# Gates in two passes, the slope by ScalarE's derivative, phases as 16-bit halves, and two sets of PSUM evictions on VectorE

## Chip, core and metric

The kernel runs on one core of a Trainium2 chip. TensorE multiplies matrices, VectorE and ScalarE work element by element, GpSimd does a little of that and issues DMAs, and SyncE issues most DMAs. The metric is device time in microseconds (us) of one execution; lower is better.

## What is computed

A forward and a backward pass over x of shape 2048 x 512 (bf16):

```python
xn = _layernorm(x)
s = _A_ref(xn, ...)            # a long convolution, kernel K from a diagonal state-space model
g = _silu(_B_ref(xn, w1, w2))  # o = silu(xn @ w1) @ w2 ; g = silu(o)
return x + s * g
```

`_A_ref` forms K[d, l] = Re sum_n C dt B exp(dt A l) for 512 channels and 2048 places, and convolves it with xn by Fourier transforms. The outputs are the result and the gradients of x, of the eight state-space parameters and of the two weights, for a given `grad_out`. For the gates the backward pass needs two things: ds = grad_out * silu(o), the gradient of the convolution's output, and do = grad_out * s * silu'(o), the gradient of the feed-forward output.

## The kernel before

The kernel is written with a tile framework. The code yields work in small steps, and generators are woven together by fixed weights (`interleave`, `woven`, `paced`). A planner then sets the order on each engine at build time, from an estimate of when each instruction's inputs and buffers are ready, with the order of the code as priority. On the chip each engine and each DMA queue works through its list in order.

The stages, by the profile's time:

- Up to about 44 us: loads, constants, layer norm. GpSimd builds the selection matrices `SEL`, ScalarE the magnitudes `mag`.
- 44 to 258 us, the table stage. `gen_tables` runs for four blocks b of 128 channels, each in two halves h. A half forms phases `V` (int32) on VectorE in two groups of 16 and 15 exponents: a product `tau * e`, a shift by a quarter turn for the cosine (L435), and a shift left by 32 - PB bits (L436), so that a turn wraps at 32 bits. ScalarE takes the sine (`sn`, L438), VectorE multiplies by `mag` into `E`, `Y` and `H`, and TensorE multiplies `Y` by `W` into `ps_k`. ScalarE evicts that to `Xr`. At the end of a block TensorE gathers `Xr` by selection matrices into two groups of `ps_e` (one PSUM buffer, pool `pt`), and twelve copies write them, some broadcast, into `KE` (`ev`, `evk`: ScalarE). Four DMAs on ScalarE's queue (L507) write `KE` to DRAM (`Kd`). The forward convolution of the block before (`gen_conv_fwd`: Kb, two Fourier stages, product with U, two inverse stages, `S_b`, stored to `Sd`) and the forward feed-forward (`gen_ffn_fwd`, in chunks of 256 rows, 0.58 steps for each step of the tables) are woven in. The feed-forward stores each chunk of o to DRAM (`Od`, by GpSimd's queue).
- 258 to about 312 us, the gate stage. The table buffers are freed; `ds` and the pool `gate` (Gr, g, u, S) take their place. The forward convolution of block 3, the last feed-forward chunk and the gates (`gen_gate_rows`, eight chunks c of 256 rows) are woven. `k.do` lies over the space of the table `Y` (the trace names it YD). A chunk whose o came while the tables still stood is loaded from `Od` into `k.do`; a chunk that comes after (`k.late`) is read from its buffer `ob`. For each chunk the gates take g = silu(o) (three buffers), store g to DRAM (`Gd`), take tanh(o/2), form ds, and build the slope from tanh and g by five VectorE instructions, then multiply by Gr and by S for blocks 0 to 2. Block 3's S_b follows at L1162.
- Meanwhile W1 and W2 are turned in place (`turned_in_place`: eight transposes in TensorE into a PSUM bank, one eviction, seven times for each). The evictions go by `evw`, pattern "AD": ScalarE and VectorE in turn.
- From about 299 us: `gen_conv_bwd`. `forward(0)` transforms ds (it needs all chunks); four steps of it are drawn before `gen_ffn_da`. Then its products (L347 to L354) with U and K, the backward feed-forward (ps_da, L925 and L927), the first output (`gen_out`), and after that the state-space gradients, the weight gradients and the layer norm's backward pass, up to 703.6 us.

The DMA buffers of the Fourier stages come by tags: `w8` (four buffers), and from the backward pass on also `w8b` (two), which take turns by a fixed cycle.

Of the kernel before, what the change touches and what calls it, by code (L numbers as in the profile page):

```python
# [10 lines left out]
ACT = mybir.ActivationFunctionType  # L11
ALU = mybir.AluOpType
F32 = mybir.dt.float32
BF16 = mybir.dt.bfloat16
I32 = mybir.dt.int32
DRAM = bass.MemoryType.DRAM
PSUM = bass.MemoryType.PSUM
P = 128
PI_LO = 3.1415925
PB = 18  # L20


BR, SR = 1.8, 0.5
# [392 lines left out]
def gen_tables(k, b):  # L416

    nc, tbl = k.nc, k.tbl
# [3 lines left out]
    for h in range(2):  # L422
        hs = slice(b * P + 64 * h, b * P + 64 * h + 64)
        mag = tbl.tile([P, NX, 64], BF16, name="mag", tag="mag")
        nc.sync.dma_start(mag[:].rearrange("p e d -> p (e d)"), k.Md[2 * b + h])
        E = tbl.tile([P, 2, 16, NE, 4], BF16, name="E", tag="E")
        Y = k.Y[h]
        H = tbl.tile([P, 2, 16, 3, 4], BF16, name="H", tag="H")
        qe = lambda ap: ap.rearrange("p e (q a) -> p e q a", a=4)
        eq = lambda ap: ap.rearrange("p q e a -> p e q a")  # L430
        for (x0, n) in ((0, 16), (16, 15)):
            V = tbl.tile([P, 2, 16, 64], I32, name="V", tag="tv", bufs=2)
            TT(out=V[:, 1, 0:n], in0=k.tau[:, hs].unsqueeze(1).to_broadcast([P, n, 64]),
               in1=k.ecst[:, x0:x0 + n].unsqueeze(2).to_broadcast([P, n, 64]), op=ALU.mult)
            TS(out=V[:, 0, 0:n], in_=V[:, 1, 0:n], scalar=-float(1 << (PB - 2)), op=ALU.add)  # L435
            TS(out=V[:, :, 0:n], in_=V[:, :, 0:n], scalar=32 - PB, op=ALU.logical_shift_left)  # L436
            sn = tbl.tile([P, 2, 16, 64], BF16, name="sn", tag="ts", bufs=2)
            nc.scalar.activation(out=sn[:, :, 0:n], in_=V[:, :, 0:n], func=ACT.Sin, scale=-2 * PI_LO / 2.0 ** 32)  # L438
            yield
            for c in range(2):  # L440
                if x0 == 0:
                    parts = ((E[:, c, :, 0:16, :], 0, 16),)
                else:
                    parts = ((E[:, c, :, 16:NE, :], 0, 5), (Y[:, c, :, 1:8, :], 5, 12), (H[:, c], 12, 15))
                for o, i0, i1 in parts:
                    TT(out=eq(o), in0=qe(sn[:, c, i0:i1]), in1=qe(mag[:, x0 + i0:x0 + i1, :]), op=ALU.mult)
                yield
        nc.sync.dma_start(k.Ed[b, h], E[:].rearrange("p c q e a -> p (c q e a)"))
# [12 lines left out]
        for q0 in range(0, 16, 8):  # L461
            W = tbl.tile([P, 4, 8, NE, 4], BF16, name="W", tag="W", bufs=2)
            g = (hs.start + 4 * q0) // 32
            for m, ec in ((0, 0), (2, 1)):
                ct = k.CT[:, g, ec:ec + 2, :].rearrange("p m (q a) -> p (m q) a", a=4).unsqueeze(2).to_broadcast([P, 16, NE, 4])
                e = E[:, ec, q0:q0 + 8].rearrange("p q e a -> p (q e a)").unsqueeze(1).to_broadcast([P, 2, 8 * NE * 4])
                TT(out=W[:, m:m + 2].rearrange("p m q e a -> p (m q) e a"), in0=e, in1=ct, op=ALU.mult)  # L467
            for u in range(2):
                ps = k.pt.tile([P, 4, 84], F32, name="ps_k", tag="pt")
                for q in range(4):  # L470
                    for m in range(4):
                        nc.tensor.matmul(out=ps[:, q], lhsT=Y[:, m % 2, q0 + 4 * u + q].rearrange("p j a -> p (j a)"),  # L472
                                         rhs=W[:, m, 4 * u + q].rearrange("p e a -> p (e a)"), start=(m == 0), stop=(m == 3))
# [10 lines left out]
                i += 1  # L484
    KE = tbl.tile([P, 8, 8, 32], BF16, name="KE", tag="W", bufs=2)
    bc = lambda ap, n: ap.unsqueeze(2).to_broadcast([P, ap.shape[1], n, 32])
    ev = k.evk
    A = k.pt.tile([P, 16, 32], F32, name="ps_e", tag="pt")
    group(A[:], [(0, 0, 16)])
    ev(KE[:, 0], A[:, 8:16])  # L490
# [61 lines left out]
def gen_ffn_fwd(k):  # L552
    nc, fp = k.nc, k.fp
    D, FT, DK, T = k.D, k.FT, k.DK, k.T
    for c in range(T // 2):
# [20 lines left out]
            yield  # L576
        if c == T // 2 - 1:
            turned_in_place(k, k.W1, k.evw)
        ob = fp.tile([P, 2, D], BF16, name="ob", tag="ob", bufs=2)
        for t in range(2):  # L580
            ps = k.pf.tile([P, D], F32, name="ps_o", tag="pf")
            for ft in range(FT):
# [1 line left out]
                                 start=(ft == 0), stop=(ft == FT - 1))  # L584
            k.evf(ob[:, t], ps[:])
            yield
        k.st(k.Od[:, 2 * c:2 * c + 2, :], ob[:])
        k.rows_done = c + 1
        if k.late:
            k.ob[c] = ob  # L590

def gen_gate_rows(k, gp, lag):

    nc = k.nc
    TT = nc.vector.tensor_tensor
    last = k.T // 2
    Gr = gp.tile([P, k.T, k.D], BF16, name="Gr")
    for t in range(0, k.T, 4):  # L600
        nc.sync.dma_start(Gr[:, t:t + 4, :], k.g_v[:, t:t + 4, :])
    for c in range(last):
        while k.rows_done <= c or (c not in k.ob and k.rows_done < min(c + 1 + lag, last)):
            yield
        ts = slice(2 * c, 2 * c + 2)
        o = k.do[:, ts, :]
        src = o
        if c in k.ob:
            src = k.ob.pop(c)[:]
        else:  # L610
            nc.sync.dma_start(o, k.Od[:, ts, :])
        G = Gr[:, ts, :]
        S = gp.tile([P, 3, 2, P], BF16, name="S", tag="S", bufs=4)
        nc.sync.dma_start(S[:].rearrange("p b t d -> p b (t d)"), k.Sd[0:3, :, 256 * c:256 * c + 256].rearrange("b p n -> p b n"))
        if src is o:
            yield
        g = gp.tile([P, 2, k.D], BF16, name="g", tag="g", bufs=3)
        nc.scalar.activation(out=g[:], in_=src, func=ACT.Silu)
        nc.sync.dma_start(k.Gd[:, ts, :], g[:])
        nc.scalar.activation(out=o, in_=src, func=ACT.Tanh, scale=0.5)  # L620
        TT(out=k.ds[:, ts, :], in0=G, in1=g[:], op=ALU.mult)

        nc.vector.tensor_scalar(out=o, in0=o, scalar1=-0.5, scalar2=0.5, op0=ALU.mult, op1=ALU.add)
        u = gp.tile([P, 2, k.D], BF16, name="u", tag="u", bufs=2)
        nc.vector.tensor_scalar(out=u[:], in0=g[:], scalar1=1.0, scalar2=-1.0, op0=ALU.mult, op1=ALU.add)
        TT(out=o, in0=o, in1=u[:], op=ALU.mult)
        nc.vector.tensor_single_scalar(out=o, in_=o, scalar=1.0, op=ALU.add)
        TT(out=o, in0=o, in1=G, op=ALU.mult)
        o3 = o[:, :, 0:3 * P].rearrange("p t (b d) -> p b t d", b=3)
        TT(out=o3, in0=o3, in1=S[:], op=ALU.mult)  # L630
        yield
# [413 lines left out]
def kernel(ctx, tc, A_u, A_A_re, A_A_im, A_B_re, A_B_im, A_C_re, A_C_im, A_log_dt, A_Dskip, B_x, B_w1, B_w2, grad_out,  # L1045
           out_0, out_1, out_2, out_3, out_4, out_5, out_6, out_7, out_8, out_9, out_10, out_11):
    nc = tc.nc
# [32 lines left out]
    k.pc = ctx.enter_context(tc.tile_pool(name="pc", bufs=2, space=PSUM))  # L1080
    k.pt = ctx.enter_context(tc.tile_pool(name="pt", bufs=1, space=PSUM))
    k.evk, k.evc, k.evf, k.evb, k.evv = (Evac(nc, "A") for _ in range(5))
    k.evx, k.evw, k.evq = Evac(nc, "D"), Evac(nc, "AD"), Evac(nc, "D")

    k.st = nc.gpsimd.dma_start
    k.const = pool("const")
# [63 lines left out]
    k.rows_done, k.late, k.ob = 0, False, {}  # L1150
    ffn = gen_ffn_fwd(k)
    paced(chain(), ffn, 0.58)
    es_t.close()
    k.late = True
    k.ds = pool("ds", side="right", es=es_x).tile([P, 16, D], BF16, name="ds")
    es_g = es_x.enter_context(ExitStack())
    gates = gen_gate_rows(k, pool("gate", side="right", es=es_g), 1)

    interleave([gen_conv_fwd(k, 3), ffn, gates], [1, 3, 1])
    for t in (slice(0, 8), slice(8, 16)):  # L1160
        last = k.do[:, t, 3 * P:4 * P]
        nc.vector.tensor_tensor(out=last, in0=last, in1=k.S_b[:, t], op=ALU.mult)  # L1162
# [4 lines left out]
    k.dftb = SimpleNamespace(tile=lambda shape, dt, name, tag: base.tile(shape, dt, name=name, tag=next(turn) if tag == "w8" else tag))  # L1167
# [48 lines left out]
```

## Time and profile before

| | before |
|---|---|
| three runs | 702.93, 706.72, 713.55 us |
| median | 706.72 us |
| span of the profiled execution | 703.6 us (no other time is listed for it) |
| busy TensorE, VectorE, ScalarE, GpSimd | 597.5, 534.5, 465.3, 85.6 us |
| mean granted TensorE clock | 0.958 |
| DMA | 148.81 MB, mean 211 GB/s |

Busy time is a share of the whole span; the stages differ much, so it has to be read stage by stage. Each row of a group of instructions gives the line, engine, operation, output and input tiles with shapes and the count, then busy us, the mean of one in ns, and the idle us of the engine just before them with what ended it. Back-to-back instructions overlap a little, so that the busy time of a full queue is less than count times mean.

### The profile page before, as it was taken

The page shows a single profiled execution, that of the slowest core. Times are in us where ns is not written, and L with a number is a line of the kernel's source. Part 1 is how long each engine was busy: PE and PEld are TensorE (multiplying, and loading weights), DVE is VectorE, ACT ScalarE, POOL GpSimd, SP SyncE. Part 2 cuts the span into 40 slices and gives each one's busy share as a digit, 9 for nine tenths or more (in the row PEclk, how much of TensorE's full clock was granted, in tenths as well). Part 3 has the DMA queues.
Part 4 walks back from the last instruction along what each step waited for, and adds up shares of the span by engine and source line. Part 5 has one row for each costly group of instructions (what it writes and reads, how often), then busy time and mean ns, then how long its engine had stood idle before and what let it go on. Part 6 is the DMA issues. An engine that isn't in the chain of part 4 may idle for free.

```text
span 703.6 us, 14464 instructions
## 1 busy us (share of the span) xinstructions
PE 597.5 (85%) x5884; PEld 436.8 (62%) x5884; DVE 534.5 (76%) x952; ACT 465.3 (66%) x626; POOL 85.6 (12%) x165
## 2 busy tenths in 40 slices
PE   0675988779999997549988999988998989999988
PEld 0454656466667675337675666756777767755877
DVE  6988995979979958999685969626679774755950
ACT  6877666779878888877664765615728665645431
POOL 2355200000000000000000000000001020123220
PEclk9998998899999999779999999999999999999999
DMA  9955453825835779598857545479989999337993
GB/s 280 342 139 201 150 192 143 329 77 211 306 120 217 288 245 310 175 295 264 275 166 226 184 172 180 129 155 226 249 202 252 197 235 232 110 116 254 288 229 99
DMA packets 158771, 148.81 MB, mean 211 GB/s; under 512 B 79280, under 2 KB 136112, under 8 KB 155120
## 3 DMA queue, kind: packets, MB, share of 16 engines
q1 hardware_dynamic: 145664, 125.07, 62.3%
q0 software_dynamic: 6144, 17.83, 6.7%
q10 hardware_dynamic: 6896, 4.98, 2.2%
q8 instruction: 46, 0.75, 0.4%
q14 instruction: 21, 0.17, 0.1%
HBM read 65.14 MB, written 64.36 MB: 184 GB/s over the span
## 4 chain that ended last, share of the span: by engine, by line
issue 74%; POOL 8%; DVE 8%; PE 4%; DMA 4%; ACT 1%; SPq 0%; POOLq 0%; DVEq 0%
PE ps_w L986 2%; POOL Hd L575 1%; DMA dh_tok<-DHd 1%; DVE st L269 1%; POOL out_dram L842 1%; POOL rstd L273 1%; DVE jk L1019 1%; POOL SEL L220 1%; DVE o L1029 1%; DMA out_dram<-gout 1%; PE ps_o L583 1%; DMA out_dram<-o 1%; DVE xn L279 1%; POOL out_dram L971 1%; PE ps_h L566 1%
## 5 line engine op out<-in xcount | busy, mean ns | idle before, releaser
L44 ACT CAST dA<-ps_s 128x1024 bf16<-128x1024 f32 x96 | 93.6, 1027 | 16.2 <-PE ps_s L298 10.2
L925 PE MATMUL ps_da<-doT,W 128*128 128x256 bf16 x448 | 62.5, 280 | 5.7 <-DVE dhT L927 5.7
L44 ACT CAST dB<-ps_i 128x1024 bf16<-128x1024 f32 x48 | 47.3, 1027 | 29.2 <-PE ps_i L327 24.4
L772 DVE TENSOR_TENSOR Tp<-Vb,Eb 128x1344 bf16<-128x1344 bf16 x64 | 51.9, 853 | 18.5 <-ACT Vb L44 7.9
L927 DVE TENSOR_TENSOR dhT<-ps_da,dhT 128x512 bf16<-128x512 f32 x56 | 37.8, 686 | 34.2 <-PE ps_da L925 29.3
L566 PE MATMUL ps_h<-XT,W 128*128 128x256 bf16 x448 | 62.1, 284 | 0.6 <-DVE XT L45 0.4
L583 PE MATMUL ps_o<-W,aT 128*128 128x512 bf16 x224 | 56.9, 390 | 3.5 <-ACT aT L574 1.6
L327 PE MATMUL ps_i<-I,sp_in 128*128 128x256 bf16 x384 | 51.4, 279 | 8.0 <-DVE sp_in L350 4.9
L936 PE MATMUL ps_dx<-W,dhT 128*128 128x512 bf16 x224 | 54.1, 379 | 0.0
L925 PEld LDWEIGHTS <-W 128*128 128x128 bf16 x448 | 43.0, 100 | 16.7 <-issue 10.8
L986 PE MATMUL ps_w<-dh_tok,xn 128*128 128x256 bf16 x448 | 49.7, 272 | 3.6 <-DMA dh_tok<-DHd 3.5
L968 PE MATMUL ps_w<-YD,a_tok 128*128 128x512 bf16 x224 | 51.5, 379 | 0.0
L566 PEld LDWEIGHTS <-W 128*128 128x128 bf16 x448 | 43.2, 102 | 12.3 <-issue 5.5
L986 PEld LDWEIGHTS <-xn 128*128 128x128 bf16 x448 | 43.6, 98 | 9.8 <-issue 4.5
L327 PEld LDWEIGHTS <-sp_in 128*128 128x128 bf16 x384 | 36.7, 100 | 20.9 <-DVE sp_in L350 8.2
L44 ACT CAST Vb<-ps_v 128x672 bf16<-128x672 f32 x64 | 42.3, 725 | 10.7 <-PE ps_v L762 10.6
L44 ACT CAST o<-ps_w 128x256 bf16<-128x256 f32 (+1 forms) x42 | 17.7, 439 | 46.4 <-PE ps_w L986 16.9
L314 PE MATMUL ps_s<-dB,F 128*64 128x512 bf16 x192 | 33.6, 418 | 12.2 <-DVE dB L45 6.5
L298 PEld LDWEIGHTS <-TF 128*128 128x128 bf16 x384 | 26.7, 102 | 24.4 <-issue 18.6
L583 PEld LDWEIGHTS <-aT 128*128 128x128 bf16 x224 | 21.3, 100 | 29.4 <-issue 9.3
L45 DVE COPY dB<-pt_f 128x2048 bf16<-128x2048 bf16 x24 | 28.7, 1218 | 12.5 <-PE pt_f L304 12.4
L472 PE MATMUL ps_k<-W,YD 128*128 128x84 bf16 x512 | 29.4, 210 | 9.6 <-DVE W L467 7.7
(231 smaller groups left out, 1304.5 us busy)
## 6 DMA issues: line engine op xcount, KB each, us to landing
Yd<-YD SPq DMA_DIRECT2D x8, 1024.0 KB, 4.5
sp_in<-Ud SPq DMA_DIRECT2D x8, 1024.0 KB, 7.4
h_in<-Hd SPq DMA_DIRECT2D x14, 512.0 KB, 4.3
Ed<-E SPq DMA_DIRECT2D x8, 672.0 KB, 4.1
Eb<-Ed SPq DMA_DIRECT2D x8, 672.0 KB, 5.2
Hd<-hT POOLq DMA_DIRECT2D x8, 512.0 KB, 6.0
Ud<-dA SPq DMA_DIRECT2D x4, 1024.0 KB, 8.1
KXd<-dA SPq DMA_DIRECT2D x4, 1024.0 KB, 5.2
```

The source lines that it names most:

```text
L44: return self.nc.scalar.copy(out=out, in_=in_)
L314: nc.tensor.matmul(out=ps[64 * h:64 * h + 64, 4 * v:4 * v + 4], lhsT=k.F2[:, c, :], rhs=Bv[:, u, h, 4 * v:4 * v + 4, :], start=True, stop= ...
L327: nc.tensor.matmul(out=ps[:, g], lhsT=Y[:, c, g0 + g, :], rhs=k.I2[:, c].rearrange("p c m -> p (c m)"), start=(c == 0), stop=(c == 1))
L472: nc.tensor.matmul(out=ps[:, q], lhsT=Y[:, m % 2, q0 + 4 * u + q].rearrange("p j a -> p (j a)"), rhs=W[:, m, 4 * u + q].rearrange("p e a - ...
L566: nc.tensor.matmul(out=ps[:, j], lhsT=k.W1[:, dk, ft * P:ft * P + P], rhs=XTv[:, :, dk, :], start=(dk == 0), stop=(dk == DK - 1))
L583: nc.tensor.matmul(out=ps[:], lhsT=aT[:, ft, t * P:t * P + P], rhs=k.W2[:, ft, :], start=(ft == 0), stop=(ft == FT - 1))
L772: k.nc.vector.tensor_tensor(out=Tp[:, c, :, r ^ c].rearrange("p e (q w) a -> p q w e a", w=2), in0=Vb[:, :, c].rearrange("p q w (e a) -> p ...
L925: nc.tensor.matmul(out=ps[:, j], lhsT=k.W2[:, ft, dk * P:dk * P + P], rhs=dTv[:, :, dk, :], start=(dk == 0), stop=(dk == DK - 1))
L927: nc.vector.tensor_tensor(out=dh[:, i0:i0 + 2, :], in0=ps[:], in1=dh[:, i0:i0 + 2, :], op=ALU.mult)
L936: nc.tensor.matmul(out=ps[:], lhsT=dhs[ft // 8][:, ft % 8, t * P:t * P + P], rhs=k.W1[:, :, ft * P:ft * P + P], start=(ft == 0), stop=(ft ...
L968: nc.tensor.matmul(out=ps[:], lhsT=at[:, t, :], rhs=k.do[:, t, :], start=(t == 0), stop=(t == k.T - 1))
L986: nc.tensor.matmul(out=ps[:], lhsT=k.xn[:, t, dk * P:dk * P + P], rhs=dh[:, t].rearrange("p j n -> p (j n)"), start=(t == 0), stop=(t == k ...
```

## The change

It does these things:

- Phases keep 16 bits for a turn (PB 18 to 16). The shift left is gone; the sine reads the low 16-bit half of each 32-bit phase.
- The twelve `KE` copies of a block go by `evw`, and `evw` is VectorE alone, so the copies of turned W1 and W2 go there too.
- Late chunks of o are evicted straight into `k.do`, and are not stored to `Od`.
- The gates are split. Pass one (`gen_gate_rows`) loads o where needed, takes g, stores it and forms ds. Pass two (`gen_slope_rows`) loads S, takes silu'(o) in place by ScalarE's Derivative_silu, and multiplies by Gr and S.
- Pass two is drawn in turn with the first four steps of the backward convolution, which now come ahead of the turning of W2. The cycle of buffers is turned by two places to match.

```diff
-PB = 18
+PB = 16
...
-            TS(out=V[:, :, 0:n], in_=V[:, :, 0:n], scalar=32 - PB, op=ALU.logical_shift_left)
+            low = V[:].bitcast(I16).rearrange("p c e (d w) -> p c e d w", w=2)[:, :, 0:n, :, 0]
...
-            nc.scalar.activation(out=sn[:, :, 0:n], in_=V[:, :, 0:n], func=ACT.Sin, scale=-2 * PI_LO / 2.0 ** 32)
+            nc.scalar.activation(out=sn[:, :, 0:n], in_=low, func=ACT.Sin, scale=-2 * PI_LO / 2.0 ** PB)
...
-    ev = k.evk
+    ev = k.evw
...
-        ob = fp.tile([P, 2, D], BF16, name="ob", tag="ob", bufs=2)
+        late = k.late
+        ob = k.do[:, 2 * c:2 * c + 2, :] if late else fp.tile([P, 2, D], BF16, name="ob", tag="ob", bufs=2)
...
-        k.st(k.Od[:, 2 * c:2 * c + 2, :], ob[:])
+        if late:
+            k.ob.add(c)
+        else:
+            k.st(k.Od[:, 2 * c:2 * c + 2, :], ob[:])
         k.rows_done = c + 1
-        if k.late:
-            k.ob[c] = ob
...
         ts = slice(2 * c, 2 * c + 2)
         o = k.do[:, ts, :]
-        src = o
-        if c in k.ob:
-            src = k.ob.pop(c)[:]
-        else:
+        if c not in k.ob:
             nc.sync.dma_start(o, k.Od[:, ts, :])
-        G = Gr[:, ts, :]
+            yield
+        g = gp.tile([P, 2, k.D], BF16, name="g", tag="g", bufs=3)
+        nc.scalar.activation(out=g[:], in_=o, func=ACT.Silu)
+        nc.sync.dma_start(k.Gd[:, ts, :], g[:])
+        nc.vector.tensor_tensor(out=k.ds[:, ts, :], in0=k.Gr[:, ts, :], in1=g[:], op=ALU.mult)
+        yield
+
+
+def gen_slope_rows(k, gp):
+
+    nc = k.nc
+    TT = nc.vector.tensor_tensor
+    for c in range(k.T // 2):
+        ts = slice(2 * c, 2 * c + 2)
+        o = k.do[:, ts, :]
         S = gp.tile([P, 3, 2, P], BF16, name="S", tag="S", bufs=4)
         nc.sync.dma_start(S[:].rearrange("p b t d -> p b (t d)"), k.Sd[0:3, :, 256 * c:256 * c + 256].rearrange("b p n -> p b n"))
-        if src is o:
-            yield
-        g = gp.tile([P, 2, k.D], BF16, name="g", tag="g", bufs=3)
-        nc.scalar.activation(out=g[:], in_=src, func=ACT.Silu)
-        nc.sync.dma_start(k.Gd[:, ts, :], g[:])
-        nc.scalar.activation(out=o, in_=src, func=ACT.Tanh, scale=0.5)
-        TT(out=k.ds[:, ts, :], in0=G, in1=g[:], op=ALU.mult)
-
-        nc.vector.tensor_scalar(out=o, in0=o, scalar1=-0.5, scalar2=0.5, op0=ALU.mult, op1=ALU.add)
-        u = gp.tile([P, 2, k.D], BF16, name="u", tag="u", bufs=2)
-        nc.vector.tensor_scalar(out=u[:], in0=g[:], scalar1=1.0, scalar2=-1.0, op0=ALU.mult, op1=ALU.add)
-        TT(out=o, in0=o, in1=u[:], op=ALU.mult)
-        nc.vector.tensor_single_scalar(out=o, in_=o, scalar=1.0, op=ALU.add)
-        TT(out=o, in0=o, in1=G, op=ALU.mult)
+        nc.scalar.activation(out=o, in_=o, func=ACT.Derivative_silu)
+        TT(out=o, in0=o, in1=k.Gr[:, ts, :], op=ALU.mult)
         o3 = o[:, :, 0:3 * P].rearrange("p t (b d) -> p b t d", b=3)
         TT(out=o3, in0=o3, in1=S[:], op=ALU.mult)
         yield
...
-    k.evx, k.evw, k.evq = Evac(nc, "D"), Evac(nc, "AD"), Evac(nc, "D")
+    k.evx, k.evw, k.evq = Evac(nc, "D"), Evac(nc, "D"), Evac(nc, "D")
...
-    gates = gen_gate_rows(k, pool("gate", side="right", es=es_g), 1)
-
-    interleave([gen_conv_fwd(k, 3), ffn, gates], [1, 3, 1])
+    gp = pool("gate", side="right", es=es_g)
+    k.dftb = SimpleNamespace(tile=lambda shape, dt, name, tag: k.dft.tile(shape, dt, name=name, tag=tag))
+    bwd = gen_conv_bwd(k)
+    interleave([gen_conv_fwd(k, 3), ffn, gen_gate_rows(k, gp, 1)], [1, 3, 1])
+    interleave([itertools.islice(bwd, 4), gen_slope_rows(k, gp)], [1, 1])
...
-    turn = itertools.cycle(["w8"] * 4 + ["w8b"] * 2)
...
+    turn = itertools.cycle(["w8"] * 2 + ["w8b"] * 2 + ["w8"] * 2)
...
     turned_in_place(k, k.W2, k.evw)
-    bwd = gen_conv_bwd(k)
     out = gen_out(k, da)
-    for i in range(4):
-        next(bwd)
```

More of the change, by code (lines that the diff above doesn't have):

```diff
@@ L15 @@
 I32 = mybir.dt.int32
+I16 = mybir.dt.int16
 DRAM = bass.MemoryType.DRAM
@@ L586, in gen_ffn_fwd @@
             yield
-        k.st(k.Od[:, 2 * c:2 * c + 2, :], ob[:])
+        if late:
+            k.ob.add(c)
+        else:
+            k.st(k.Od[:, 2 * c:2 * c + 2, :], ob[:])
         k.rows_done = c + 1
-        if k.late:
-            k.ob[c] = ob
 def gen_gate_rows(k, gp, lag):
     nc = k.nc
-    TT = nc.vector.tensor_tensor
     last = k.T // 2
-    Gr = gp.tile([P, k.T, k.D], BF16, name="Gr")
+    k.Gr = gp.tile([P, k.T, k.D], BF16, name="Gr")
     for t in range(0, k.T, 4):
-        nc.sync.dma_start(Gr[:, t:t + 4, :], k.g_v[:, t:t + 4, :])
+        nc.sync.dma_start(k.Gr[:, t:t + 4, :], k.g_v[:, t:t + 4, :])
     for c in range(last):
@@ L1149, in chain @@
             yield from woven([gen_tables(k, b), gen_conv_x(k, b), gen_conv_fwd(k, b - 1)], [3, 1, 1])
-    k.rows_done, k.late, k.ob = 0, False, {}
+    k.rows_done, k.late, k.ob = 0, False, set()
     ffn = gen_ffn_fwd(k)
@@ L1165 @@
     base = dft_pool("dftb", es_x, {"cm2": 1, "xd": 1, "w8b": 2}, k.dft, side="right")
-    turn = itertools.cycle(["w8"] * 4 + ["w8b"] * 2)
-    k.dftb = SimpleNamespace(tile=lambda shape, dt, name, tag: base.tile(shape, dt, name=name, tag=next(turn) if tag == "w8" else tag))
+    turn = itertools.cycle(["w8"] * 2 + ["w8b"] * 2 + ["w8"] * 2)
+    k.dftb.tile = lambda shape, dt, name, tag: base.tile(shape, dt, name=name, tag=next(turn) if tag == "w8" else tag)
     da = pool("da", es=es_d)
     turned_in_place(k, k.W2, k.evw)
-    bwd = gen_conv_bwd(k)
     out = gen_out(k, da)
-    for i in range(4):
-        next(bwd)
     ffb = gen_ffn_da(k, da)
```

## Prediction

> **What bounds the kernel now.** I read the page first, then the waits, then a table of stretches, then the groups of VectorE and ScalarE by shape, and last the order of time from 255 to 352 us. TensorE is busy for 597.5 of 703.6 us and VectorE for 534.5, so neither is the bound everywhere; the stretches say where each is.
>
> ```profile
> DVE  6988995979979958999685969626679774755950
> PEclk9998998899999999779999999999999999999999
> ...
> 44.00:160.00 116.00, 92.39 (x933) 66.11 (x931) 96.89 (x134) 82.68 (x117) 25.73 (x29) 0.91 0.47 169
> 160.00:258.00 98.00, 94.48 (x1029) 67.17 (x1026) 88.62 (x120) 87.08 (x125) 8.60 (x11) 1.00 0.65 235
> 258.00:280.00 22.00, 17.79 (x208) 13.21 (x208) 15.53 (x26) 18.26 (x21) 0.57 (x1) 0.98 0.85 272
> 280.00:312.00 32.00, 17.02 (x143) 12.08 (x140) 31.75 (x59) 25.84 (x25) 0.00 (x0) 0.71 0.71 225
> 312.00:341.00 29.00, 25.97 (x256) 19.14 (x254) 27.41 (x39) 21.35 (x24) 2.20 (x4) 0.98 0.83 269
> 341.00:703.60 362.60, 331.97 (x3219) 247.48 (x3218) 238.38 (x471) 197.22 (x269) 35.58 (x64) 0.98 0.76 198
> ```
>
> In the stretches the columns after the length are the busy us of TensorE, its weight loads, VectorE, ScalarE and GpSimd, then the granted clock. From 280 to 312 us VectorE is busy for 31.75 of 32 us while TensorE has 17.02, at a clock of 0.71: this is the gate stage, and VectorE bounds it. From 160 to 258 us TensorE has 94.48 of 98 and bounds. After 341 us TensorE has 331.97 of 362.6, and what begins earlier there ends earlier.
>
> ```profile
> L436 DVE TENSOR_SCALAR V<-V 128x2048 int32<-128x2048 int32 x8 | 9.9, 1231 | 0.0
> L436 DVE TENSOR_SCALAR V<-V 128x1920 int32<-128x1920 int32 x8 | 9.3, 1165 | 0.0
> L626 DVE TENSOR_TENSOR YD<-YD,u 128x1024 bf16<-128x1024 bf16 x8 | 5.5, 684 | 0.0
> L630 DVE TENSOR_TENSOR YD<-YD,S 128x768 bf16<-128x768 bf16 x8 | 4.4, 551 | 1.6 <-DMA S<-Sd 1.6
> L625 DVE TENSOR_SCALAR u<-g 128x1024 bf16<-128x1024 bf16 x8 | 3.4, 420 | 0.0
> L623 DVE TENSOR_SCALAR YD<-YD 128x1024 bf16<-128x1024 bf16 x8 | 3.4, 419 | 0.0
> L627 DVE TENSOR_SCALAR YD<-YD 128x1024 bf16<-128x1024 bf16 x8 | 3.4, 419 | 0.0
> ...
> L620 ACT ACTIVATE YD<-YD 128x1024 bf16<-128x1024 bf16 x7 | 7.2, 1062 | 0.0
> L44 ACT CAST KE<-ps_e 128x128 bf16<-128x128 f32 x12 | 3.3, 342 | 0.0
> L902 ACT ACT_TABLE_LOAD x1 | 1.3, 1283 | 0.0
> ```
>
> These are the instructions that the change takes away or moves. The order of time shows how the stage ends:
>
> ```profile
> 273.38 1.08 ACT L620 ACTIVATE YD<-ob 128x1024 bf16<-128x1024 bf16 x1
> ...
> 296.78 1.07 ACT L618 ACTIVATE g<-ob 128x1024 bf16<-128x1024 bf16 x1
> ...
> 304.91 0.69 DVE L621 TENSOR_TENSOR ds<-Gr,g 128x1024 bf16<-128x1024 bf16 x1
> ...
> 318.28 0.69 DVE L347 TENSOR_TENSOR cm<-sp_in,dA 128x1024 bf16<-128x1024 bf16 x1 [1.22 <-ACT dA L44]
> ```
>
> Only one chunk is late (one `g<-ob`). Its tanh runs 23 us ahead of its silu: the planner puts whatever it holds ready first, and the silu waits for one of three g buffers. The last ds comes at 304.91, though its silu was done by 298 at the latest; ds stands in VectorE's full queue. The backward transform needs all of ds, and its first product (L347) comes at 318.28.
>
> **The change part by part.** Prices on VectorE are from start to start in a full queue: the 0.42 us form comes every 0.33 (285.38 to 285.71), the 0.68 us form every 0.60, the shift every 1.10 (a pair from 72.66, next start 74.86).
>
> *Gates.* Each of eight chunks loses L623, L625, L626 and L627: 3 x 0.33 + 0.60 = 1.6, so 12.9 us of VectorE, all in the stage that it bounds. What stays is ds, one multiply by Gr, one by S. Tanh becomes Derivative_silu: L902 takes 1913 ns for 2048 and 1492 for 1536 elements, so 1071 for 1024, against 1062: nothing. The eight loads of S (192 KB each, SP's queue) move behind all of pass one. In the old order each stood ahead of the store of its g, and the first had to wait for Sd of block 2; now Gd goes out sooner and g comes free sooner. VectorE's 1.6 us wait for S goes too: at that time it will have ds and W copies, and S loads run during the forward transform. If that cover fails, the 1.6 stays. S has four buffers, so the fifth load waits for L630 of the first chunk, and behind it on SP stand sp_in, dhT and go_g, wanted by ScalarE and VectorE only after 305; I give this nothing, with up to 3 us (half the median landing of S, 6.1) as upper end. The forward transform of block 0 now needs pass one alone, so it can overlap the tail of block 3's forward convolution.
>
> *Late o.* One chunk: two evictions go to their final place, one 256 KB store (L587, 0.57 us of GpSimd issue) is gone. GpSimd is idle in the stage (0.57 of 54 us), so nothing.
>
> *Turned weights.* Seven copies leave ScalarE (7.1 us, 1031 ns each) for VectorE at 0.60. Four are of W1, around 250 to 263 us, where VectorE waits 3.07 and 4.16 us for TensorE: no cost. Three are of W2 in the gate stage: +1.8.
>
> *Phases.* The shift goes: 16 x 1.10 = 17.6 us of VectorE. The first two are worth nothing, since VectorE then waits 1.5 us for GpSimd's SEL before YD; 14 x 1.10 = 15.4. The Sin now reads every second 16-bit word. No row shows that; ScalarE takes 1943 ns for 2048 int32 and 1923 for 2048 bf16 (L574), the nearest rows, so I take no change. Upper end: twice as long is 30 us of ScalarE, and it idles 44 us from 44 to 258; up to 10 us might show. A gain is not excluded but has no row; 0.
>
> *Selection results.* 48 copies (KE, 15.2 us) leave ScalarE for VectorE. VectorE's nearest rows that read PSUM are 686 ns for 512 and 1220 for 1024 elements: 152 ns plus 1.04 an element. For 8192 elements in 48 copies that is 15.8 us busy, about 12 start to start. Lower end, by the fp32 copy of 218 ns for 128 elements from SBUF (L818): 8 us. I take 12, since the source is PSUM. So the table stage has 3.4 us less of VectorE and 15 less of ScalarE. Here a wait is added twice: VectorE's queue stands when ps_e is not ready, and what stands behind it is the next block's V and E, for which Sin and ps_k wait; and the four Kd issues on ScalarE's queue now wait for VectorE, with Sin and hT evictions behind. As TensorE has 94.48 of 98 us in the second half, I count 2.5 us gained; ends: 7 gained, and the third rival.
>
> *Sum.* Gate stage: -12.9 - 1.6 + 1.8 = -12.7. ScalarE is next: 25.84 of 32 us busy, and it keeps its silu and slope work, about 40 us from 262 on, so it could end near 304; I give back 0.7, so -12. Table stage -2.5. Together -14.5. The span gives 703.6 - 14.5 = 689.1; the span lies near the lower of the three runs (702.93, 706.72, 713.55), and 14.5 off their median is **692.2**.
>
> **Rivals.** *Table switches eat half.* The planner holds the slope of chunk 0 ready as soon as its silu is done, while later silus wait for g buffers; the early tanh above shows that it then pulls a ready instruction ahead. Silu, Tanh and Sin alternate without a load now, and Derivative_silu needed one (L902). Each return trip costs 2 x 1283 ns of ScalarE; three trips are 7.7 us in a stage where ScalarE is next to bound: 700. Against it: g comes free sooner, and ScalarE has evictions to fill. The Trainium skill, in "ScalarE: Activation LUTs", section "Table sets: the hidden batching unit", says to do all of one set before switching, and puts a switch at some 2.7 us with its drain; the row here has 1.28 and the next start 0.23 later. By the page three trips would be 16 us and the gain gone.
>
> *The clock comes back.* At 280 to 312 us TensorE's 17.02 us of work ran at 0.71. With shorter pauses at full clock it would be 12.1, and if ScalarE then ends the stage at its floor near 304, the stage gives 5 to 6 us more: 686. For it: the clock is 1.00 wherever TensorE is kept busy. Against: ScalarE, not TensorE, comes next. The Trainium skill, "TensorE: Matmul & The Clock Gate", section "What's actually happening", ties a half clock to an idle window of about 3.4 us; the trace agrees so far that pauses of 3.7 us (288.19) and 3.1 (309.34) stand in that stretch.
>
> *VectorE stands for the selection (slower).* In block 3 the last product W ends at 246.4, the first ps_e ends at 253.6 and the last KE copy at 258.1. If the planner puts the copies right behind W, VectorE stands through 253.6 - 246.4 = 7.2 us for each of four blocks, 29 us: 692.2 + 29 = 721. It turns slower than before from 3.6 us a block. Against it: the trace has V, shifts, E and cplx products between the two, and the planner orders by readiness; for it: both ps_e groups share one PSUM buffer.
>
> **How the numbers follow.** The forecast has 0.60, with its own range 685 to 699; the clock 0.18; switches 0.10; the standing queue 0.12. A 2% step, about what a measurement of this kernel can tell from no change, is 14.1 us, so the border is 692.6. The forecast lies at it: of its 0.60 I put 0.33 beyond and 0.27 within. Faster 0.33 + 0.18 = 0.51, same 0.27 + 0.10 = 0.37, slower 0.12. The range 679 to 712 reaches below the second rival by the 7 us end of the selection, and above the first by the ends of the S loads and the Sin; most of the third stays outside.
>
> **What would show it.** Right: no L623 to L627; the last ds before 290 us instead of 304.9; the first bwd L347 near 304 to 307 instead of 318; VectorE below 90% in that stage and ScalarE above 90%; one load of Derivative_silu's table; KE copies on VectorE at about 290 ns for 128 elements; Sin at 1.9 us; 341 to the end no longer than 363 us. Wrong: more than one such load, VectorE waiting over 3 us for ps_e, Sin well over 1.94, or a tail after the gate stage that gives the gain back.

## The result and the profile after

The changed kernel takes 702.21 us (median of 20 runs) against 706.53 us for the kernel before (20 runs): a ratio of 0.9936, 95% interval 0.9907 to 0.9965, or 4.5 us (2.5 to 6.6). The forecast was 14.5 us. All ratios here compare fast runs alone, those at most 1.5% above the fastest of the same kernel, so a ratio need not be that of the two medians. The profiled execution has a span of 700.7 us against 703.6, busy TensorE 596.9 us, VectorE 519.8, ScalarE 453.9, and a mean granted clock of 0.961.

The table of stretches, with the columns of the one shown before:

```profile
44.00:160.00 116.00, 97.15 (x1038) 71.24 (x1037) 104.67 (x164) 82.87 (x100) 22.48 (x30) 0.94 0.53 190
160.00:258.00 98.00, 94.39 (x974) 65.28 (x971) 77.41 (x127) 76.81 (x96) 7.69 (x10) 1.00 0.62 221
258.00:280.00 22.00, 14.22 (x180) 10.66 (x177) 16.84 (x24) 19.21 (x22) 0.00 (x0) 0.95 0.78 264
280.00:312.00 32.00, 24.43 (x231) 18.52 (x231) 28.03 (x44) 30.58 (x31) 0.56 (x1) 0.82 0.90 294
312.00:341.00 29.00, 22.96 (x184) 15.06 (x181) 19.15 (x28) 16.53 (x18) 1.66 (x3) 0.88 0.71 218
```

Three rows carry the story. From 280 to 312 us VectorE falls from 31.75 to 28.03 us and TensorE rises from 17.02 to 24.43, but ScalarE is now at 30.58 of 32. From 312 to 341 every engine has *less* to do than before (TensorE 22.96 after 25.97, VectorE 19.15 after 27.41): something stands there. And from 44 to 160, VectorE has become fuller, 104.67 after 96.89, although the shift is gone.

The groups of the moved instructions, by shape:

```profile
L439 ACT ACTIVATE sn<-V 128x2048 bf16<-128x2048 int16 x8 | 15.4, 1930 | 2.5 <-DVE V L436 2.5
L628 ACT ACTIVATE YD<-YD 128x1024 bf16<-128x1024 bf16 x8 | 8.3, 1058 | 0.0
L628 ACT ACT_TABLE_LOAD x3 | 3.8, 1283 | 0.1
L46 DVE CAST KE<-ps_e 128x128 bf16<-128x128 f32 x12 | 3.0, 276 | 0.0
L613 ACT ACT_TABLE_LOAD x2 | 2.6, 1283 | 1.3 <-DMA Gd<-g 1.3
```

The prices of single instructions are as forecast: the sine of 16-bit halves takes 1930 ns for 2048 elements (1943 for 32-bit words before), the derivative 1058 ns, the KE copy of 128 elements 276 ns on VectorE. But the tables of ScalarE are loaded five times around silu and its derivative, not once. The order of time at the end of the gates:

```profile
286.87 1.06 ACT L613 ACTIVATE g<-YD 128x1024 bf16<-128x1024 bf16 x1
...
287.96 0.69 DVE L615 TENSOR_TENSOR ds<-Gr,g 128x1024 bf16<-128x1024 bf16 x1
...
289.76 1.28 ACT L628 ACT_TABLE_LOAD   x1
...
297.95 1.07 ACT L628 ACTIVATE YD<-YD 128x1024 bf16<-128x1024 bf16 x1
...
303.03 0.55 DVE L631 TENSOR_TENSOR YD<-YD,S 128x768 bf16<-128x768 bf16 x1
...
305.31 1.28 DVE L928 TENSOR_TENSOR dhT<-ps_da,dhT 128x512 bf16<-128x512 f32 x2
```

The lines are the last silu, the last ds, the last load, the last derivative, the last slope product with S and the first product of the backward feed-forward. The last ds comes at 287.96 (304.91 before), the last slope product at 303.03 (310.00 before), that first product, dhT, at 305.31 (318.89 before). At that point the changed kernel leads by 13.6 us. At the end of the span it leads by 2.9. Between the two lies a hole; the timeline after the gates shows it (idle time before an instruction, and what ended it, in brackets):

```profile
331.44 0.69 DVE L657 TENSOR_TENSOR go_x<-go_x,go_g 128x1024 bf16<-128x1024 bf16 x1 [4.62 <-DMA go_x<-in_A_u_dram]
...
334.53 0.40 PE L328 MATMUL ps_i<-I,sp_in 128*128 128x256 bf16 x1 [4.65 <-DVE sp_in L351]
...
337.10 1.01 ACT L45 CAST dB<-ps_i 128x1024 bf16<-128x1024 f32 x1 [7.58 <-PE ps_i L328]
...
342.34 0.69 DVE L657 TENSOR_TENSOR go_x<-go_x,go_g 128x1024 bf16<-128x1024 bf16 x1 [6.47 <-DMA go_x<-in_A_u_dram]
```

The first output is formed chunk by chunk in go_x, which has one buffer: the load of the next chunk waits until the store of the last has left. Here the store is issued at 332.43 us and takes 4.2 us in the median; the next load is issued at 336.98, and the sum that needs it starts at 342.34. VectorE stands 4.6 and 6.5 us for these loads. Behind the waiting instruction in its queue are the backward products of sp_in; TensorE waits for those, and ScalarE for TensorE. Before, VectorE also waited for this buffer (4.0 us), but TensorE had 13.84 us of work from 330 to 344; after, it has 9.47.

### The profile page after: what moved, and what is told of

Same layout as the page of the kernel before. It is cut to its first block, busy times and chain, and to the rows that moved or that the text cites. A ratio compares the mean times of both kernels' runs of the same rounds, so it can differ in the third digit from the quotient of the medians.

```text
span 700.7 us, 14417 instructions
## 1 busy us (share of the span) xinstructions
PE 596.9 (85%) x5884; PEld 437.0 (62%) x5884; DVE 519.8 (74%) x959; ACT 453.9 (65%) x575; POOL 80.9 (12%) x164
## 5 line engine op out<-in xcount | busy, mean ns | idle before, releaser
L45 ACT CAST dA<-ps_s 128x1024 bf16<-128x1024 f32 x96 | 93.4, 1034 | 14.5 <-PE ps_s L299 11.9
L926 PE MATMUL ps_da<-doT,W 128*128 128x256 bf16 x448 | 60.3, 275 | 6.0 <-DVE dhT L928 3.9
L987 PE MATMUL ps_w<-dh_tok,xn 128*128 128x256 bf16 x448 | 51.2, 278 | 5.4 <-DMA dh_tok<-DHd 5.4
L926 PEld LDWEIGHTS <-W 128*128 128x128 bf16 x448 | 42.1, 98 | 16.3 <-issue 11.5
L299 PEld LDWEIGHTS <-TF 128*128 128x128 bf16 x384 | 26.1, 101 | 20.6 <-issue 15.0
L315 PE MATMUL ps_s<-dB,F 128*64 128x512 bf16 x192 | 30.5, 388 | 6.9 <-ACT dA L45 2.6
```

Source lines behind the costliest of these rows:

```text
L45: return self.nc.scalar.copy(out=out, in_=in_)
L315: nc.tensor.matmul(out=ps[64 * h:64 * h + 64, 4 * v:4 * v + 4], lhsT=k.F2[:, c, :], rhs=Bv[:, u, h, 4 * v:4 * v + 4, :], start=True, stop= ...
L926: nc.tensor.matmul(out=ps[:, j], lhsT=k.W2[:, ft, dk * P:dk * P + P], rhs=dTv[:, :, dk, :], start=(dk == 0), stop=(dk == DK - 1))
L987: nc.tensor.matmul(out=ps[:], lhsT=k.xn[:, t, dk * P:dk * P + P], rhs=dh[:, t].rearrange("p j n -> p (j n)"), start=(t == 0), stop=(t == k ...
```

## The experiments

Each compares its kernel with the kernel before, run on the same chip in the same set of runs; the ratios are those. The median of the kernel before moved between 704.3 and 707.6 us from one set to the next, so kernels of different sets are compared by ratio.

**The two kernels again.** No edit.

> The kernel before, unchanged, once more. In the two profiles in hand the changed kernel leads by 9.5 us at the last dhT (L927, 519.1 against 509.6 us) and by 2.9 at the end, though from there on the instructions stand in the same order on every engine. Theory spread: the stretch from the last dhT to the end (184.5 us before, 191.1 after) varies by several us from execution to execution of one kernel, and the profile of before had a short one; here it is 186 to 192. Theory give-back: something in that stretch takes the lead back each time; here it is 184 to 186 again. Time 706 +- 3 by both.

Measured: 707.57 us, ratio 0.9974 (0.993 to 1.0018).

> The changed kernel, unchanged, once more. Spread: last dhT near 509.6 again, and the stretch behind it anywhere from 184 to 192 us. Give-back: the stretch is 189 to 193 again, longer than in the kernel before by 4 or more. Time 702 +- 3 by both.

Measured: 702.23 us, ratio 0.9908 (0.9864 to 0.9951); in a later set, beside three of its variants:

> The changed kernel itself, beside its three variants on one chip. It came at 702.2 in two sets, so 702 is expected here too, 0.991 to 0.994 of before. If the variants differ from it only because they ran in other sets, it comes at 695 to 697 like them; then neither the switches nor KE's move cost anything that the end sees.

Measured: 701.45 us, ratio 0.9935 (0.9898 to 0.9972). The changed kernel is 4 to 6 us faster. A quarter of a per cent, 2 us, is what the same kernel shows against itself here, and half a per cent further below, where one kernel has 0.9852 in one set and 0.9904 in another; smaller differences between sets say nothing. The stretch behind the last dhT, 191.1 us in the first trace of the changed kernel, is 184.4 in the third (184.5 before): it varies from execution to execution, as theory spread has it.

**The change cut in two.** First the new gates alone, on the changed kernel with shift, 18 bits and the evictions as before:

```diff
-PB = 16
+PB = 18
...
-    ev = k.evw
+    ev = k.evk
...
-    k.evx, k.evw, k.evq = Evac(nc, "D"), Evac(nc, "D"), Evac(nc, "D")
+    k.evx, k.evw, k.evq = Evac(nc, "D"), Evac(nc, "AD"), Evac(nc, "D")
```

> The changed kernel with the old phases (shift, PB 18), KE on ScalarE and turned weights on both engines: the gates, late o and the buffer cycle alone. If the gate stage makes the lead (theory gates), the last dhT comes 6 to 9 us before 519.1 and the time is 3 to 8 below the kernel before. If the lead is mostly the table stage's (theory tables), under 4 us at the last dhT and no time that can be told from before.

Measured: 706.88 us, ratio 1.0009 (0.9973 to 1.0044): nothing. Then the rest alone, put on the kernel before (16-bit phases, KE and turned weights on VectorE, old gates):

> The kernel before with 16-bit phases, KE and turned weights on VectorE, and the old gates. Theory gates: 1 to 4 us of lead at the start of block 3's forward convolution, and since the turned weights add to VectorE in the gate stage, 0 to 3 at the last dhT; time within 3 of before. Theory tables: 5 us or more at the last dhT, and 3 to 5 in time.

Measured: 709.18 us, ratio 1.0028 (0.9992 to 1.0065): nothing either. Neither half brings the 4 to 6 us of the whole. The timeline of the new gates alone shows why they bring nothing:

```profile
303.32 0.69 DVE L1165 TENSOR_TENSOR YD<-YD,S_b 128x1024 bf16<-128x1024 bf16 x1
304.18 1.07 ACT L628 ACTIVATE YD<-YD 128x1024 bf16<-128x1024 bf16 x1
305.13 2.84 ACT L45 COPY W<-pt_t 128x1024 bf16<-128x1024 bf16 x3
...
323.91 1.28 DVE L928 TENSOR_TENSOR dhT<-ps_da,dhT 128x512 bf16<-128x512 f32 x2
```

ScalarE takes the derivative of the last chunk at 304.18 and only then copies the turned W2 that the backward feed-forward needs: ds is 11 us earlier than before (294.3 after 304.9), yet ScalarE comes to `doT`, the transposed do that the first dhT also needs, only at 318.95. The first dhT comes at 323.9, later than the 318.9 of before.

The rest alone is ahead by 6.5 us at the last KE copy, by 7.0 at the first dhT and by 2.7 at the last one (516.4 after 519.1); what it gains in the table stage it loses behind the gates.

**Only the four VectorE instructions.** The kernel before without the lines that build the slope:

```diff
-        nc.vector.tensor_scalar(out=o, in0=o, scalar1=-0.5, scalar2=0.5, op0=ALU.mult, op1=ALU.add)
-        u = gp.tile([P, 2, k.D], BF16, name="u", tag="u", bufs=2)
-        nc.vector.tensor_scalar(out=u[:], in0=g[:], scalar1=1.0, scalar2=-1.0, op0=ALU.mult, op1=ALU.add)
-        TT(out=o, in0=o, in1=u[:], op=ALU.mult)
-        nc.vector.tensor_single_scalar(out=o, in_=o, scalar=1.0, op=ALU.add)
```

> The kernel before without the four VectorE instructions L623 and L625 to L627 of each gate chunk (the slope is left out, tanh times grad_out stands in its place); silu and tanh keep one table. It prices these 12.9 us of a full VectorE by themselves. Theory that VectorE bounds the gate stage: first dhT 9 to 13 us earlier, at 306 to 310, and 6 to 11 us in time. Theory that the next bound takes most: first dhT 3 to 7 earlier, time within 4 of before.

Measured: 701.52 us, ratio 0.9987 (0.9944 to 1.0031). The last ds comes 6.5 us earlier, the first dhT 5.3 (313.6), the end of the backward convolution 2.1. In the time nothing can be told from zero, but the interval reaches from 4 us faster to 2 us slower, and by the medians (706.01 for the kernel before) it would be 4.5 us. The stretch of the stage:

```profile
280.00:312.00 32.00, 19.68 (x153) 13.62 (x153) 25.36 (x39) 26.64 (x27) 0.00 (x0) 0.68 0.83 266
```

VectorE falls from 31.75 to 25.36 us, and no engine is full: what was 12.9 us of a full engine is 5 to 6 us of path.

**The table switches.** The changed kernel with each derivative ordered behind the last silu:

```diff
+        k.last_silu = nc.cur_bb.bb.instructions[-1]
...
-        nc.scalar.activation(out=o, in_=o, func=ACT.Derivative_silu)
+        with k.tc.issue_after(k.last_silu):
+            nc.scalar.activation(out=o, in_=o, func=ACT.Derivative_silu)
```

> The changed kernel, with every Derivative_silu of pass two queued behind the last silu of pass one, so that ScalarE loads the table once there. Theory switches: the four extra loads of 1.28 us cost ScalarE 5.1 us in the gate stage; the first dhT comes 3 to 6 us earlier and the time falls by 2 to 5. Rival: slope work moved behind the last silu is late by as much as the loads took, or go_x takes the rest; first dhT within 2 us of 305.3 and time within 2 of 702.

Measured: 696.49 us, ratio 0.9852 (0.9804 to 0.99). Again, beside the changed kernel itself:

> The changed kernel with every slope instruction behind the last silu, again. If the four extra table loads (5.1 us of ScalarE at the end of the gates) reach the end, it stays at 696 to 698, 5 us below the changed kernel of the same set. If the difference to 702 was that of the sets, it comes within 1.5 us of the changed kernel here.

Measured: 697.47 us, ratio 0.9904 (0.9872 to 0.9936), 4.0 us below the 701.45 of the changed kernel in that set; by the ratios of that set it is 2.2 us, by those of the two first sets 5.9 (0.9852 against 0.9936). One load is left of the five:

```profile
L630 ACT ACT_TABLE_LOAD x1 | 1.3, 1283 | 0.0
```

Four loads of 1.28 us are 5.1 us of ScalarE, and 2 to 6 us come out of the time. That the loads are what the time gains is not shown. The two derivatives that end the row of eight and the first dhT of the first of these two kernels:

```profile
299.71 2.00 ACT L630 ACTIVATE YD<-YD 128x1024 bf16<-128x1024 bf16 x2
...
308.20 0.69 DVE L930 TENSOR_TENSOR dhT<-ps_da,dhT 128x512 bf16<-128x512 f32 x1
```

The last derivative ends at 301.7 instead of 299.0, because all eight now wait for the last silu, and the first dhT comes at 308.2, and at 306.3 in the second run, against 305.3 and 306.9 in two traces of the changed kernel. On that point the rival was right. The lead comes further back, where VectorE's two waits for go_x are 2.3 and 2.4 us (2.2 and 1.7 in the second run) instead of 4.6 and 6.5. The same edit on the new gates alone:

> The gates alone, as in the run before (old phases, KE on ScalarE, turned weights on both engines), with every Derivative_silu queued behind the last silu. With the gates alone ScalarE had five loads of 1.28 us and three turned weights of 1 us in the gate stage, and the first dhT came at 323.9 us, later than in before (318.9), though the last ds came 10.6 us earlier. Theory ScalarE: the split hands the stage from VectorE to ScalarE, so 5.1 us less there bring the first dhT to 316 to 320 and the time to 699 to 704. Rival: ScalarE's loads fill pauses, and neither moves by more than 2 us.

Measured: 703.02 us, ratio 0.9952 (0.9917 to 0.9986), first dhT at 309.6 instead of 323.9. So the new gates by themselves are worth 3 to 4 us in this order, and nothing in the planner's. The 14.3 us at the first dhT are more than 5.1 us of loads: with the derivatives held back, the last copies of turned W2 come before 284 us instead of from 305 to 311.

**The buffer go_x.** The sum of the first output is written into go_g and stored from there, so that go_x is free as soon as it is read:

```diff
-        TT(out=x[:], in0=x[:], in1=g[:], op=ALU.add)
-        k.st(k.o0_v[:, 2 * c:2 * c + 2, :], x[:])
+        TT(out=g[:], in0=x[:], in1=g[:], op=ALU.add)
+        k.st(k.o0_v[:, 2 * c:2 * c + 2, :], g[:])
```

> The changed kernel, with the first output's sum written over go_g instead of go_x, so that the one go_x buffer is free after the sum and not after its store. Theory go_x: in the changed kernel the lead over before is 13.6 us at the first dhT and 9.9 at the fourteenth, and between them VectorE waits 4.6 and 6.5 us for go_x with the products behind it that TensorE needs; each new load has to wait for a store of some 4 us. Then these waits fall under 3 us in all, the lead at the fourteenth dhT grows by 4 to 8 us, and the time falls by 3 to 7 against the changed kernel, to about 697. Theory spread: the loss there differs between executions anyway, and the time stays within 2 of 702.

Measured: 695.16 us, ratio 0.9858 (0.981 to 0.9905). VectorE's waits for go_x fall to 2 us in all, as theory go_x has it, but the fourteenth dhT, at 357.8 us, is not earlier than in the first trace of the changed kernel (357.4; 364.0 in another).

> Both edits together. If go_x and switches are both on the path their gains add: 5 to 11 us below the changed kernel, 691 to 697. If go_x alone: as the kernel with the sum in go_g, 696 to 699. If neither: 700 to 704.

Measured: 694.95 us, ratio 0.9846 (0.9805 to 0.9887).

> The kernel before, with the sum over go_g. In before VectorE waits 4.0 us for go_x and 2.2 for go_g at 341 to 349, where TensorE has work for the whole 10 us. Theory go_x as a wait that the earlier gate stage uncovered: here the edit gives 0 to 2 us. Rival: go_x costs before as much as after, and the edit gives 3 to 7 here too.

Measured: 706.68 us, ratio 1.0004 (0.9972 to 1.0035). On the kernel before it does nothing, as TensorE had other work there. On the changed kernel it brings 3.5 to 5.5 us by the ratios of other sets (0.9858 against 0.9908 to 0.9936); the changed kernel was not run in this one. Within the set, the buffer alone (0.9858), the order of the derivatives alone (0.9852) and both (0.9846) cannot be told apart. So the two edits do not add. With go_x free, taking the four loads away as well brings nothing that can be told (695.16 to 694.95 us), which speaks against the loads as the price in the changed kernel; what both edits take away, the hole at go_x or something in the order behind it, the runs do not settle.

**The phases.** The changed kernel with 18 bits and the shift again:

> The changed kernel with the shift of the phases back (PB 18). It puts 17.6 us of VectorE into the table stage. Theory VectorE in the table stage: Kd's DMAs and with them block 3's forward convolution come 4 to 8 us later, the first dhT 3 to 7 later, time 704 to 709. Theory TensorE there: under 3 us at both, time within 3 of 702.

Measured: 707.29 us, ratio 1.0017 (0.9985 to 1.005). The shift costs the whole gain. And the kernel before with nothing but the 16-bit phases:

```diff
-PB = 18
+PB = 16
...
-            TS(out=V[:, :, 0:n], in_=V[:, :, 0:n], scalar=32 - PB, op=ALU.logical_shift_left)
+            low = V[:].bitcast(I16).rearrange("p c e (d w) -> p c e d w", w=2)[:, :, 0:n, :, 0]
...
-            nc.scalar.activation(out=sn[:, :, 0:n], in_=V[:, :, 0:n], func=ACT.Sin, scale=-2 * PI_LO / 2.0 ** 32)
+            nc.scalar.activation(out=sn[:, :, 0:n], in_=low, func=ACT.Sin, scale=-2 * PI_LO / 2.0 ** PB)
```

> Before with the 16-bit phases alone: no shift on VectorE (17.6 us less), everything else as before. If the shift is worth what the changed kernel loses when it comes back (ratio 0.9936 to 1.0017, 5.7 us), it comes at 0.992 of before. If the gates stage of before takes the lead back (its VectorE is full either way), 0.998 to 1.002, with the last ds still 4 to 6 us earlier than 304.9. The forecast's price for the shift was up to 15 us.

Measured: 697.01 us, ratio 0.9878 (0.9812 to 0.9943): this part alone brings nearly twice what the whole change brings (8.6 us, with 4 to 13 inside the interval). The last sine starts 11.7 us earlier (223.1 after 234.8), the last KE copy 11.5 (246.2 after 257.7), the first dhT 16.3 (302.6). The first stretch of this kernel:

```profile
44.00:160.00 116.00, 100.98 (x1046) 72.86 (x1044) 96.53 (x136) 92.04 (x128) 23.32 (x30) 0.94 0.54 190
```

TensorE does 100.98 us of work there against 92.39 before. VectorE is as busy as before (96.53): it spends what the shift had taken on work that comes earlier.

**The selection results.** The changed kernel with the KE copies back on ScalarE:

```diff
-    ev = k.evw
+    ev = k.evk
```

> The changed kernel with the selection results (KE) on ScalarE again; turned weights stay on VectorE. Theory that the move to VectorE cost what I counted (12 us of VectorE, 15 us less of ScalarE, a gain on balance): 0 to 3 us slower than the changed kernel. Theory that it costs more than it gives, since VectorE was the fuller engine in the table stage: 1 to 5 us faster than the changed kernel, with the last KE copy before 250 us (251.8 there).

Measured: 696.50 us, ratio 0.9857 (0.9822 to 0.9893): 0.8% below the changed kernel by the ratios of two sets, 5.6 us. The last KE copy starts at 245.3 us instead of 251.7. And the kernel before with the copies on VectorE:

> Before with the 48 selection copies on VectorE alone. If the move is a loss of its own, as the changed kernel without it says (5.6 us), it comes at 1.006 to 1.010 of before, the last ds at 309 or later. The forecast's price was 12 us on VectorE against 15 off ScalarE, all but a few us of it behind TensorE: then 1.000, and the last ds near 305.

Measured: 707.59 us, ratio 1.0026 (0.9994 to 1.0059). On the kernel before the move costs 1.8 us, with zero inside the interval, and the last ds comes at 304.2, not at 309 or later; on the changed kernel it costs 5.6. The stretch of 140 to 160 us, in the changed kernel and then with KE on ScalarE, shows where:

```profile
140.00:160.00 20.00, 14.34 (x186) 12.97 (x187) 18.01 (x25) 10.91 (x14) 1.46 (x2) 0.83 0.54 185
```

```profile
140.00:160.00 20.00, 19.25 (x221) 15.44 (x220) 14.85 (x22) 17.37 (x21) 1.59 (x3) 1.00 0.51 185
```

TensorE loses 4.9 us there, as much as in all of 44 to 245 us (180.11 of work after 184.94). The waits of TensorE in that stretch, changed kernel, and of VectorE with KE on ScalarE (us in total, times, longest):

```profile
PE ps_s L299 <- DVE S_b L545: 4.1, 1, 4.1
```

```profile
DVE S_b L545 <- PE ps_i L337: 6.7, 1, 6.7
```

The same eviction, `S_b`, in two roles. With KE on ScalarE, VectorE is waiting for the product that S_b reads. With KE on VectorE, the next transform (L299), which takes its PSUM buffer over, waits for VectorE, which is busy without a gap:

```profile
146.42 0.95 DVE L459 TENSOR_TENSOR YD<-m,m 128x1536 bf16<-128x1536 bf16 x1
147.29 0.85 DVE L468 TENSOR_TENSOR W<-E,CT 128x1344 bf16<-128x1344 bf16 x1
148.06 1.21 DVE L545 TENSOR_TENSOR S_b<-ps_i,xd 128x1024 bf16<-128x1024 f32 x1
...
149.32 1.01 PE L299 MATMUL ps_s<-xn,TF 128*128 128x128 bf16 x8 [4.07 <-DVE S_b L545]
```

The twelve KE copies before it are over by 136.7 us and take 3.7 us, less than the 6.7 us that VectorE has to spare there. What differs besides is the order: with KE on ScalarE the planner has put `S_b` ahead of the table products YD, m and W of that half, with KE on VectorE behind them.

**Both losses taken away.** KE on ScalarE and the derivatives behind the last silu, then the sum in go_g as well:

> The changed kernel with the selection results back on ScalarE and every slope instruction behind the last silu. Each alone came at 696.5, 5.7 us below 702.2. If the two losses are separate and both reach the end, the two together come at 690 to 692. If each only buys a better place in the same later stretch (the wait for go_x, then the weight gradients), the two together come at 695 to 697 again.

Measured: 690.90 us, ratio 0.9805 (0.9764 to 0.9846), 10.5 us below the changed kernel (701.45) and 6.6 below the kernel without switches (697.47), all three of one set.

> All three: selection results on ScalarE, slope instructions behind the last silu, and the first output's sum written into go_g, so that go_x comes free with the sum. If the three losses of 5.7 to 7 us add, 684 to 688; if the lead of the gate stage is capped later by something else, 693 to 696, as the pair without KE's move (694.95).

Measured: 691.65 us, ratio 0.9789 (0.975 to 0.9829): the buffer adds nothing once the other two are gone. The planner's order of the derivatives and the move of KE are separate losses, and they add. The two edits together are the version that beats both kernels, by 13.4 us the kernel before.

## Why the prediction was wrong

The sign was right, and so was the direction of VectorE's and ScalarE's load over the whole span; the size was off by 10 us. Most of the signs named for being right came true: the last ds before 290 us, the first L347 at 307.25 (L348 there), VectorE at 88% and ScalarE at 96% of the stage, KE copies of 276 ns, a sine of 1.93 us, 359.7 us from 341 to the end. These signs watch single instructions, loads of engines and the start of the path; none of them shows how much reaches the end. At the first dhT the lead is 13.6 us, near the 14.5 of the sum, but by luck: the table stage gave 6.0 where the sum has 2.5, and the gate stage 7.6 where it has 12. And the lead does not hold to the end.

**Gate stage, -12: mis-sized.** The prices of the instructions hold, and the 1.6 us wait for S is gone. The step that failed is "in the stage that it bounds", with only 0.7 given back to ScalarE. Taking the four instructions out alone is worth 5.3 us at the first dhT and nothing that can be told from zero at the end. The whole of the new gates is worth 3 to 4 us with the derivatives behind the last silu, and nothing without. I followed ds (17 us earlier, as forecast), but in VectorE's queue dhT stands behind the slope's last product, which moves only from 310.0 to 303.0, and 6.0 of these 7.0 us are the lead of the table stage. VectorE waits 1.28 us for the last derivative, and makes two copies of the transform, for which it waits 0.9 us for TensorE, before that product.

**Table stage, -2.5: both terms mis-sized.** I capped it at 2.5 because TensorE has 94.48 of 98 us from 160 to 258, and did not read the row above it: from 44 to 160 TensorE had 23.6 us of idle time. The 15.4 us that I priced for the shift went 11.5 to 11.7 deep into the path, and 8.6 us (1.22%) into the time. Against that, KE on VectorE cost 5.6 to 6.6 beside 16-bit phases. I let 12 us of VectorE be hidden behind TensorE, and 15 us of ScalarE count as a gain; the runs show the contrary, a TensorE that waits for VectorE. Net, the last KE copy is 6.0 us earlier (251.7 after 257.7).

**The tail, "what begins earlier there ends earlier": failed in part.** From the first dhT to the end of the span it is 384.7 us before, 395.4 after, 386.2 with the derivatives behind the last silu, 392.0 with KE on ScalarE. A lead of 17.1 us at the seventh dhT (of 56) is 9.9 at the fourteenth; the hole at go_x lies between. The list of signs named "a tail after the gate stage that gives the gain back" among what would make it wrong. How much of the loss is the hole is not settled: of 10.7 us, 4.1 lie between the first and the last dhT and 6.6 behind it, where from 450 us on the order on every engine is the same before and after; in another execution of the changed kernel (span 701.0) all 9.4 lie between the first and the last dhT. The same list of instructions gives its lead back in different places.

**The rivals.** *Table switches eat half* came true in the loads, with two return trips and not three, 5.1 us instead of 7.7, and 2 to 6 us of time come back when an order takes them away. I had named what would cause them, the early tanh of the trace before, and gave it one chance in ten. But that the loads cost this time is not shown: without them the first dhT is no earlier, and beside the freed go_x the same edit brings nothing. The Trainium skill, "ScalarE: Activation LUTs", section "Table sets: the hidden batching unit", says to do all calls of one set before those of the next; the kernel that does so is the faster one here. By the Trainium skill's price of about 2.7 us a switch, an estimate for the four is 11 us, but a load takes 1283 ns in the trace and the next instruction starts 0.01 us behind it, 5.1 us in all. *The clock* came back in part: 0.71 to 0.82 from 280 to 312 us. *VectorE stands for the selection* did not happen: no wait of VectorE for ps_e shows in the table stage. The damage of the move went the other way, a VectorE that is late for TensorE. *The sine* is as forecast; *late o* was not run alone.

**The sum from the runs.** Phases -8.6, KE +5.6 to +6.6, gates with the derivatives held back -3.4, the planner's order of them +4.0: together -1.4 to -2.4, against -4.5 measured, near enough for intervals of 2 to 5 us on each. But the prices depend on each other. The move of KE puts the last KE copy 5.0 to 6.4 us back where the phases have 16 bits (246.2 to 251.2, 245.3 to 251.7), and nothing to speak of where the shift stands (257.7 to 258.4, 258.8 to 257.8): it takes back about half of what the phases give. One piece does not fit: phases, KE and turned weights on the kernel before gave +2.0 (1.0028), where the parts give -2 to -3, and -7 with the price that KE has on that kernel. The turned weights were not run alone, but the trace does not put the loss on them in the gate stage: the lead is 6.7 us at the last ds and 7.0 at the first dhT, and goes from there on, with VectorE waiting 3.2 and 5.7 us for go_x. Why it goes stays open.

## What to carry to other kernels

Read every stretch of a stage before you cap a saving: an engine that is full in the second half says nothing of the first. When a full engine is relieved, size the gain by taking the work out alone, as the next engine and the chain between them decide: 12.9 us of a full VectorE were 5 us of path, and between nothing and 4 us of time. And move work off an engine only towards one that is idle *when* the work comes: the copies of KE fitted VectorE's average, but they made another eviction late for TensorE. With a planner that takes whatever is ready, try an explicit order that keeps functions of different tables apart; and when it is faster, look whether the loads or the new order did it.

## What the hardware showed beyond that

- The sine reads every second 16-bit word at the rate of whole 32-bit words: 1930 ns against 1943 for 2048 elements.
- The derivative of silu does not share its table with silu, while silu, sine and tanh alternate without a load; a change costs 1283 ns, and in the gate stage the next instruction starts 0.01 us after its end (289.76 + 1.28, then 291.05).
- For small copies out of PSUM, VectorE is the quicker engine by little: 276 ns against 333 on ScalarE for 128 elements (342 in the kernel before), but 609 against 538 for 448.
